# Softmax of grouped heads laid out by token tile, with folds in place of reduces and a direct SBUF spread; the last transpose of the first stage moved behind the paired Q chunks

## The chip, the cores and the metric

The kernel runs on one core of one Trainium2 chip. The metric is the device time of one execution in microseconds (us), as a median or mean of several executions.

Engine names: PE is TensorE (PEld its weight load), DVE is VectorE, ACT is ScalarE, POOL is GpSimd, SP is SyncE. An L number is a line of the kernel. L93 is a wrapper through which nearly all DVE, ACT and POOL operations pass, so these are told apart by their tile names. L118 holds nearly all matmuls; L213 (L219 in the changed kernel) holds those that transpose tiles. PSUM is the memory that matmuls write their sums to; an eviction is the DVE or ACT operation that reads such a sum out of it, so that the accumulator can be used again. The granted clock is the share of PE's full clock that the trace records.

## The reference

Two layers are applied to x of 2048 tokens by 1024 columns in bf16. Each is an attention block followed by a feed-forward block.

```
x = x + A(layernorm(x))     # 32 heads of 32; a query at s sees keys s, s-2, ..., s-14 (window 8, dilation 2)
                            # logits with negative key positions are -1e9; softmax over the 8; times V; times Wo
x = x + B(layernorm(x))     # gelu(x @ w1 + b1) @ w2 + b2, 1024 -> 3584 -> 1024
(both once more, with the same weights)
```

## The kernel before

The tokens go through in groups of 512, four per layer. The eight (layer, group) pairs are n = 0 to 7. For each n there are a QKV stage, a Wo stage and two FFN stages, all of them matmuls. They are interleaved so that DVE can do the attention of group n+2 while PE does the matmuls of group n. PE's program order is forced. `hold()` makes every later DVE instruction follow all that DVE was given up to now.

The first stage (n = 0) starts while its inputs still arrive. Four layer-norm tiles of 128 tokens must be transposed on PE. Tiles 2 and 3 come late, between paired Q chunks that need only tiles 0 and 1:

```python
# gen_qkv, n == 0: six chunks, each summed over k in four quarters kq, on tokens 0..255
for kq in range(4 if n == 0 else 0):
    for c in range(6):
        first[c] = qkv_chunk(wq, c, xnT, first.get(c), kq * (KD // 4), (kq + 1) * (KD // 4), 0, 2)
        if kq == 3:
            act.copy(qT[:, c, 0:2 * P], first[c][:, 0:2 * P])
        if (kq, c) in ((2, 5), (3, 1)):
            transpose_on_pe(*first_late.pop(0))     # 8 PE transposes into PSUM tile L, one ACT copy of 1024 columns
```

From group 2 on, the window logits of all heads are gathered by DMA into a tile with 128 partitions, partition = token tile * 32 + head. DVE then does the softmax. The weights `a` go to DRAM and come back spread over the head's dimensions:

```python
def gather(n):
    for tb in range(NTT):                                   # 4 transfers, each onto 32 partitions
        pool.dma_start(Lq[tb * H:(tb + 1) * H, :, :, :], prod[:, tb, :, :])

def attend(n):
    ...                                                     # e = sum of the four parts, 3 adds; mask where n % NG == 0
    vec.tensor_reduce(out=mx[:], in_=L[:].rearrange("p w t -> p t w"), axis=AX.X, op=ALU.max)
    vec.tensor_tensor(out=e[:], in0=L[:], in1=<mx for all w>, op=ALU.subtract)
    act.activation(e[:], e[:], ACT.Exp, scale=SCALE)
    vec.tensor_reduce(out=z[:], in_=e[:].rearrange("p w t -> p t w"), axis=AX.X, op=ALU.add)
    vec.reciprocal(z[:], z[:])
    vec.tensor_tensor(out=a[:], in0=e[:], in1=<z for all w>, op=ALU.mult)

def spread(n):
    for tb in range(NTT):
        pool.dma_start(a_d[:, :, tb * P:(tb + 1) * P], a[tb * H:(tb + 1) * H, :, :])   # SBUF -> DRAM
    for j in range(HP):
        pool.dma_start(abc[j::HP, :, :], a_d[:, :, :])                                 # DRAM -> SBUF

def av(n, c):          # abc * window of V, then three adds that fold 8 -> 4 -> 2 -> 1
    ...

# the stages from group 1 on (cut)
for n in range(1, N - 2):
    stage(gen_wo(n), ...)
    stage(gen_qkv(n + 2), sides=(at(0, spread, 2) if n == 1 else []) + each(av, n + 1, 0, 2, 0, 3))
    gather(n + 2)
    stage(gen_ffn1(n), ...)
    if n + 3 < N:
        stage(gen_ffn2(n), sides=at(0, attend, n + 2) + at(2, ln_a, n + 3))
    ...
```

The FFN2 stage sums four token tiles of one half of the output columns, then four of the other half. There are six PSUM accumulators, so the third tile of the second half needs that DVE has evicted the first tile of the first half.

## Time and profile before

| before | |
|---|---|
| time, median of 3 | 1233.33 us (1233.09 to 1233.33) |
| profiled span | 1231.1 us, granted clock 1.0 |
| PE busy | 1226.2 us (100%) |
| DVE busy | 870.0 us (71%) |

These are lines of the profile's page of before: busy time per engine, HBM traffic, the shares of the chain of work that ended last, and two groups of DMA transfers (count, size of one, median us from issue to landing).

```profile
PE 1226.2 (100%) x5789; PEld 632.7 (51%) x5789; DVE 870.0 (71%) x892; ACT 307.1 (25%) x491; POOL 123.0 (10%) x230
...
HBM read 197.40 MB, written 6.29 MB: 165 GB/s over the span
...
PE 99%; DVE 0%; DMA 0%; ACT 0%; issue 0%
...
abc<-a_d POOLq DMA_DIRECT2D x32, 256.0 KB, 5.0
big<-big POOLq DMA_DIRECT2D x24, 256.0 KB, 7.0
```

PE is the limit. One FFN stage is 224 matmuls of 512 columns in 48.35 us, 215.8 ns each. A group's matmuls come to 704 such units, so all eight groups need 8 x 704 x 0.2158 = 1215.4 us. This is an estimate from the trace, and the profiled span of the kernel before is only 1.3% above it. The Trainium skill, "TensorE: Matmul & The Clock Gate", section "Back-to-back issue gap", gives N/2.4 + 2.5 ns for a warm gap, 216 ns at N = 512, and the trace agrees.

The table of waits of before (engine and tile, what it waited for: us in total, times, longest us) leaves PE two:

```profile
DVE big L93 <- DMA abc<-a_d: 23.7, 2, 12.6
...
PE acc L118 <- DVE big L93: 1.1, 1, 1.1
...
PE L L213 <- ACT xnT L93: 0.7, 1, 0.7
```

The 1.1 us is the very first matmul waiting for its zeroed operand. The 0.7 us is the wait in the head of the kernel that the change goes for. It stands in the timeline of PE (start, duration, operation and count, in brackets the idle time before it and what ended that):

```profile
12.79 0.61 PE L213 MATMUL L<-ident,xn 128*128 128x128 bf16 x8
13.24 0.61 PE L118 MATMUL acc<-xnT,wt 128*128 128x256 bf16 x4
14.50 0.61 PE L213 MATMUL L<-ident,xn 128*128 128x128 bf16 x8 [0.66 <-ACT xnT L93]
14.94 2.90 PE L118 MATMUL acc<-xnT,wt 128*128 128x256 bf16 x25
```

Tile 2 is transposed at 12.79. Four chunk matmuls follow, and then the transposes of tile 3 must wait, because ACT has not yet copied tile 2 out of the PSUM tile L that both share. In the timeline of ACT, that copy runs from 13.44 to 14.45:

```profile
13.44 1.01 ACT L93 COPY xnT<-L 128x1024 bf16<-128x1024 bf16 x1 [0.97 <-PE L L213]
```

The groups of DVE instructions by shape (busy us, mean ns of one) show the two reduces of a softmax at 1.92 us each:

```profile
L93 DVE TENSOR_REDUCE z<-e 128x128 f32<-128x1024 f32 x8 | 15.4, 1926 | 33.7 <-ACT e L93 33.7
...
L93 DVE TENSOR_REDUCE mx<-e 128x128 f32<-128x1024 f32 x6 | 11.5, 1918 | 0.1
```

Four lines of the timeline of DVE before: two are the end of group 2's softmax and the first use of its spread weights. The other two are the start of the softmax in the first FFN2 stage with one, and that stage's first eviction:

```profile
281.54 1.20 DVE L93 TENSOR_TENSOR a<-e,z 128x1024 bf16<-128x1024 f32 x1
295.38 2.29 DVE L93 TENSOR_TENSOR big<-abc,vT 128x4096 bf16<-128x4096 bf16 x1 [12.64 <-DMA abc<-a_d]
...
365.65 1.22 DVE L93 TENSOR_TENSOR e<-big 128x1024 f32<-128x1024 bf16 x1
...
374.00 0.68 DVE L93 TENSOR_TENSOR tmp<-acc,b2bc 128x512 f32<-128x512 f32 x1
```

### The profile page before, as it was taken

The numbers are of one execution on the slowest core, as the hardware profiler recorded it, in microseconds if no ns is written. First come the engines' busy times: TensorE is split into PE (matmuls) and PEld (weight loads), VectorE is DVE, ScalarE is ACT, GpSimd is POOL, SyncE is SP. The second block draws the span as 40 slices with busy tenths as digits, with TensorE's granted clock in tenths as the row PEclk, the third lists the DMA queues.
The fourth block names the chain that finished last, engine by engine and source line by source line (L and its number), as shares of the span: only waits on it lengthen the run. The fifth ranks groups of instructions, "written<-read, shape, count | busy, mean of one in ns | idle before, by whom it ended". The sixth has DMA issues, their size and how long they took to land.

```text
span 1231.1 us, 13996 instructions
## 1 busy us (share of the span) xinstructions
PE 1226.2 (100%) x5789; PEld 632.7 (51%) x5789; DVE 870.0 (71%) x892; ACT 307.1 (25%) x491; POOL 123.0 (10%) x230
## 2 busy tenths in 40 slices
PE   9999999999999999999999999999999999999999
PEld 7666544456444564445544465444654444444444
DVE  8989899995996999376992779927599698012001
ACT  4343152014310143202431024310244101400310
POOL 3010011101021102200031000210000102000000
PEclk9999999999999999999999999999999999999999
DMA  9954677756487658756476565766666569546441
GB/s 301 289 179 142 177 220 183 210 140 230 147 197 226 177 165 180 220 170 186 149 187 222 172 171 169 174 222 196 171 183 157 186 200 198 166 158 196 153 136 53
DMA packets 219359, 226.63 MB, mean 184 GB/s; under 512 B 68562, under 2 KB 187488, under 8 KB 216224
## 3 DMA queue, kind: packets, MB, share of 16 engines
q1 hardware_dynamic: 214704, 208.69, 57.1%
q0 software_dynamic: 4592, 17.05, 5.7%
q8 instruction: 45, 0.74, 0.2%
q14 instruction: 18, 0.15, 0.0%
HBM read 197.40 MB, written 6.29 MB: 165 GB/s over the span
## 4 chain that ended last, share of the span: by engine, by line
PE 99%; DVE 0%; DMA 0%; ACT 0%; issue 0%
PE acc L118 99%; DMA x<-in_A_x_dram 0%; DVE stats L93 0%; PE acc L213 0%; PE L L118 0%; PE L L213 0%; ACT xnT L93 0%; DVE xn L93 0%; DVE x L93 0%; DVE mv L93 0%; PE acc L183 0%; DVE rstd L93 0%
## 5 line engine op out<-in xcount | busy, mean ns | idle before, releaser
L118 PE MATMUL acc<-xnT,wt 128*128 128x512 bf16 (+1 forms) x3392 | 720.8, 375 | 0.0
L118 PEld LDWEIGHTS <-wt 128*128 128x128 bf16 x3392 | 400.3, 119 | 318.8 <-issue 1.6
L118 PE MATMUL acc<-wt,hT 128*128 128x512 bf16 (+1 forms) x1820 | 388.1, 376 | 0.0
L118 PEld LDWEIGHTS <-hT 128*128 128x128 bf16 x1820 | 178.1, 98 | 209.0
L93 DVE TENSOR_TENSOR big<-big 128x2048 bf16<-128x2048 bf16 (+2 forms) x184 | 245.6, 1360 | 2.9
L93 ACT ACTIVATE hT<-acc,b1T 128x512 bf16<-128x512 f32 x224 | 152.5, 688 | 331.3 <-PE acc L118 331.2
L93 DVE TENSOR_TENSOR big<-qT,kT 128x4096 bf16<-128x4096 bf16 x64 | 143.8, 2286 | 26.7 <-ACT kT L93 26.1
L93 DVE TENSOR_TENSOR big<-abc,vT 128x4096 bf16<-128x4096 bf16 x64 | 144.8, 2287 | 24.3 <-DMA abc<-a_d 23.7
L93 DVE TENSOR_TENSOR tmp<-acc,b2bc 128x512 f32<-128x512 f32 x56 | 38.7, 690 | 148.4 <-PE acc L118 144.9
L93 ACT CAST qT<-acc 128x512 bf16<-128x512 f32 (+1 forms) x72 | 38.0, 542 | 341.4 <-PE acc L118 341.4
L118 PE MATMUL acc<-wt,oT 128*128 128x512 bf16 x448 | 97.9, 379 | 0.0
L93 DVE BATCH_NORM_STATS2 stats<-x 128x6 f32<-128x512 bf16 x128 | 83.5, 680 | 3.3 <-DMA x<-in_A_x_dram 2.6
L118 PEld LDWEIGHTS <-oT 128*128 128x128 bf16 x448 | 43.9, 98 | 52.8
L93 DVE TENSOR_TENSOR x<-acc,big 128x512 bf16<-128x512 f32 (+1 forms) x9 | 5.7, 633 | 90.0 <-PE acc L118 90.0
L93 POOL TENSOR_TENSOR rstd<-mv,eps_t 128x1 f32<-128x1 f32 x56 | 22.5, 402 | 434.4 <-DVE mv L93 434.3
L93 ACT CAST vT<-acc 128x512 bf16<-128x512 f32 x64 | 37.5, 586 | 83.1 <-PE acc L118 83.1
L93 ACT CAST kT<-acc 128x512 bf16<-128x512 f32 x64 | 37.3, 588 | 66.7 <-PE acc L118 66.6
L93 DVE TENSOR_TENSOR x<-acc,x 128x512 bf16<-128x512 f32 x64 | 42.6, 669 | 3.9 <-PE acc L118 3.8
L93 POOL TENSOR_TENSOR rstd<-rstd,mhalf 128x1 f32<-128x1 f32 x56 | 41.6, 743 | 4.4
L93 DVE TENSOR_SCALAR xn<-x,mv,rstd 128x1024 bf16<-128x1024 bf16 x52 | 28.4, 546 | 17.1 <-POOL rstd L93 16.9
L93 DVE TENSOR_TENSOR x<-tmp,x 128x512 bf16<-128x512 f32 x56 | 38.6, 690 | 1.6
L93 DVE TENSOR_REDUCE z<-e 128x128 f32<-128x1024 f32 x8 | 15.4, 1926 | 33.7 <-ACT e L93 33.7
(64 smaller groups left out, 252.0 us busy)
## 6 DMA issues: line engine op xcount, KB each, us to landing
wt<-in_B_w_dram SPq DMA_DIRECT2D x56, 1024.0 KB, 7.1
wt<-in_B_w_dram SPq DMA_DIRECT2D x64, 896.0 KB, 5.1
wt<-in_A_wqkv_dram SPq DMA_DIRECT2D x46, 1024.0 KB, 5.7
wt<-in_A_wo_dram SPq DMA_DIRECT2D x16, 1024.0 KB, 5.0
abc<-a_d POOLq DMA_DIRECT2D x32, 256.0 KB, 5.0
big<-big POOLq DMA_DIRECT2D x24, 256.0 KB, 7.0
x<-in_A_x_dram SPq DMA_DIRECT2D x16, 256.0 KB, 5.7
out_dram<-x SPq DMA_DIRECT2D x31, 128.0 KB, 2.4
```

Of the source, the lines that this page charges most:

```text
L93: inst = f(*args, **kwargs)
L118: return pe(nc.tensor.matmul(*args, **kwargs))
```

## The change

The intent is to take work and waits off DVE, the DMA queues and DRAM, and to close PE's gap in the head. The core of the diff (helpers and declarations are cut):

```diff
# 1. the head
@@ gen_qkv
-                if kq == 3:
-                    act.copy(qT[:, c, 0:2 * P], first[c][:, 0:2 * P])
-                if (kq, c) in ((2, 5), (3, 1)):
+                if (kq, c) in ((2, 5), (3, 5)):
+                    for done in range(2 if kq == 3 else 0):
+                        act.copy(qT[:, done, 0:2 * P], first[done][:, 0:2 * P])
                     transpose_on_pe(*first_late.pop(0))
+        for c in list(first)[2:]:
+            act.copy(qT[:, c, 0:2 * P], first[c][:, 0:2 * P])
# 2. partition = head * 4 + token tile, from group 2 on
@@ gather
-        for tb in range(NTT):
-            pool.dma_start(Lq[tb * H:(tb + 1) * H, :, :, :], prod[:, tb, :, :])
+        for j in range(HP):
+            pool.dma_start(Lq[:, j, :, :], prod[j::HP, :, :, :])
# 3. folds in place of reduces
+    def fold(e, op):
+        t = iop.tile([P, W // 2, P], F32, name="tmp")
+        vec.tensor_tensor(out=t[:], in0=e[:, 0:4, :], in1=e[:, 4:8, :], op=op)
+        vec.tensor_tensor(out=t[:, 0:2, :], in0=t[:, 0:2, :], in1=t[:, 2:4, :], op=op)
+        vec.tensor_tensor(out=t[:, 0, :], in0=t[:, 0, :], in1=t[:, 1, :], op=op)
+        return t[:, 0, :]
@@ attend
-        vec.tensor_reduce(out=mx[:], ...)                  # n < 2 keeps this one, which reads PSUM
+            mx = fold(L, ALU.max)
-        vec.tensor_reduce(out=z[:], ...)
-        vec.reciprocal(z[:], z[:])
+        vec.reciprocal(z[:], fold(e, ALU.add))
# 4. the spread, directly from SBUF to SBUF from group 2 on
@@ spread
+        if n < 2:
+            a_d = dram.tile(...)                           # groups 0 and 1 as before
+            ...
+            a = a_d
         for j in range(HP):
-            pool.dma_start(abc[j::HP, :, :], a_d[:, :, :])
+            pool.dma_start(abc[j::HP, :, :, :], a[:])
@@ av: abc is [P, NTT, W, P] now, so the adds are strided
-        vec.tensor_tensor(out=pv[:, 0:4, :], in0=pv[:, 0:4, :], in1=pv[:, 4:8, :], op=ALU.add)
+        vec.tensor_tensor(out=pv[:, :, 0:4, :], in0=pv[:, :, 0:4, :], in1=pv[:, :, 4:8, :], op=ALU.add)
# 5. one more hold
-            stage(gen_ffn2(n), sides=at(0, attend, n + 2) + at(2, ln_a, n + 3))
+            stage(gen_ffn2(n), sides=at(0, hold) + at(0, attend, n + 2) + at(2, ln_a, n + 3))
```

More of the change, by code (lines that the diff above doesn't have):

```diff
@@ L155 @@
     smat = const.tile([P, H], BF16, name="smat")
-    mask = const.tile([H, W - 1, HALO], F32, name="mask")
+    mask = const.tile([P, W - 1, HALO], F32, name="mask")
     khalo = const.tile([P, NCH, HALO], BF16, name="khalo")
@@ L171, in build_constants, with spread_mask @@
         for w in range(W - 1):
-            pool.memset(mask[:, w, 0:HALO - DIL * w], -1e9)
+            pool.memset(mask[0:H, w, 0:HALO - DIL * w], -1e9)
+    def spread_mask():
+        first = smp.tile([H, W - 1, HALO], F32, name="mx")
+        vec.tensor_copy(first[:], mask[0:H, :, :])
+        vec.memset(mask[:], 0.0)
+        pool.dma_start(mask[0::NTT, :, :], first[:])
     b1_rows = attp.tile([KF, P], BF16, name="abc")
@@ L267, in new_xnT @@
         return (pool or xnp).tile([P, NTT, KD, P], BF16, name="xnT")
-    def win(t_ap):
-        a = t_ap.ap
-        assert len(a) == 2 and a[1][0] == 1 and a[1][1] == HALO + T
-        return bass.AP(tensor=t_ap.tensor, offset=t_ap.offset, ap=[list(a[0]), [DIL, W], [1, T]])
     def win_by_tile(t_ap):
@@ L404, in attend @@
         if n % NG == 0:
-            vec.tensor_tensor(out=L[0:H, 0:W - 1, 0:HALO], in0=L[0:H, 0:W - 1, 0:HALO], in1=mask[:], op=ALU.add)
-        mx = smp.tile([P, P], F32, name="mx")
-        vec.tensor_reduce(out=mx[:], in_=L[:].rearrange("p w t -> p t w"), axis=AX.X, op=ALU.max)
-        vec.tensor_tensor(out=e[:], in0=L[:], in1=mx[:].unsqueeze(1).to_broadcast([P, W, P]), op=ALU.subtract)
+            p = H if n == 0 else P
+            vec.tensor_tensor(out=L[0:p, 0:W - 1, 0:HALO], in0=L[0:p, 0:W - 1, 0:HALO], in1=mask[0:p, :, :], op=ALU.add)
+        if n < 2:
+            mx = smp.tile([P, P], F32, name="mx")
+            vec.tensor_reduce(out=mx[:], in_=L[:].rearrange("p w t -> p t w"), axis=AX.X, op=ALU.max)
+            mx = mx[:]
+        else:
+            mx = fold(L, ALU.max)
+        vec.tensor_tensor(out=e[:], in0=L[:], in1=mx.unsqueeze(1).to_broadcast([P, W, P]), op=ALU.subtract)
         act.on = 1 < n < N - 1
@@ L412, in attend @@
         z = smp.tile([P, P], F32, name="z")
-        vec.tensor_reduce(out=z[:], in_=e[:].rearrange("p w t -> p t w"), axis=AX.X, op=ALU.add)
-        vec.reciprocal(z[:], z[:])
+        vec.reciprocal(z[:], fold(e, ALU.add))
         a = smp.tile([P, W, P], BF16, name="a")
@@ L422, in spread @@
         a = s.pop("a")
-        abc = attp.tile([P, W, T], BF16, name="abc")
+        abc = attp.tile([P, NTT, W, P], BF16, name="abc")
         s["abc"] = abc
         s["oT"] = attp.tile([P, NCH, T], BF16, name="qT" if n == N - 1 else "oT")
-        a_d = dram.tile([H, W, T], BF16, name="a_d")
-        for tb in range(NTT):
-            pool.dma_start(a_d[:, :, tb * P:(tb + 1) * P], a[tb * H:(tb + 1) * H, :, :])
+        if n < 2:
+            a_d = dram.tile([H, NTT, W, P], BF16, name="a_d")
+            for tb in range(NTT):
+                pool.dma_start(a_d[:, tb, :, :], a[tb * H:(tb + 1) * H, :, :])
+            a = a_d
         for j in range(HP):
-            pool.dma_start(abc[j::HP, :, :], a_d[:, :, :])
+            pool.dma_start(abc[j::HP, :, :, :], a[:])
     def av(n, c):
         s = st[n]
-        pv = bigp.tile([P, W, T], BF16, name="big")
-        vec.tensor_tensor(out=pv[:], in0=s["abc"][:], in1=win(s["vT"][:, c, :]), op=ALU.mult)
-        vec.tensor_tensor(out=pv[:, 0:4, :], in0=pv[:, 0:4, :], in1=pv[:, 4:8, :], op=ALU.add)
-        vec.tensor_tensor(out=pv[:, 0:2, :], in0=pv[:, 0:2, :], in1=pv[:, 2:4, :], op=ALU.add)
-        vec.tensor_tensor(out=s["oT"][:, c, :], in0=pv[:, 0, :], in1=pv[:, 1, :], op=ALU.add)
+        pv = bigp.tile([P, NTT, W, P], BF16, name="big")
+        vec.tensor_tensor(out=pv[:], in0=s["abc"][:], in1=win_by_tile(s["vT"][:, c, :]), op=ALU.mult)
+        vec.tensor_tensor(out=pv[:, :, 0:4, :], in0=pv[:, :, 0:4, :], in1=pv[:, :, 4:8, :], op=ALU.add)
+        vec.tensor_tensor(out=pv[:, :, 0:2, :], in0=pv[:, :, 0:2, :], in1=pv[:, :, 2:4, :], op=ALU.add)
+        o = s["oT"][:, c, :].rearrange("p (b t) -> p b t", t=P)
+        vec.tensor_tensor(out=o, in0=pv[:, :, 0, :], in1=pv[:, :, 1, :], op=ALU.add)
     def gen_wo(n):
@@ L594 @@
         stage(gen_qkv(n + 2), sides=(at(0, spread, 2) if n == 1 else []) + each(av, n + 1, 0, 2, 0, 3))
+        if n == 1:
+            spread_mask()
         gather(n + 2)
```

## The prediction

> **What bounds it.** TensorE. The busy table gives PE 1226.2 of 1231.1 us, the chain of waits is 99% PE matmuls, and the table of waits shows only two PE waits: 1.1 us at the start and 0.7 us before 14.50 us. In the timeline the 224 matmuls of 512 columns of one FFN half take 48.35 us (502.48 to 550.83), 216 ns each. The Trainium skill, "TensorE: Matmul & The Clock Gate", Part 2, has a matmul stream one column a cycle; 512 columns at its 2.4 GHz are 213 ns, and the trace agrees to about 1%. The change leaves the matmuls as they are, so shorter DVE, ACT or DMA work can gain no more than PE's gaps.
>
> **Head (on the chain).** PE waits 0.66 us for the ACT copy of tile 2 (13.44-14.45) before it may transpose tile 3. After the change PE first runs all twelve matmuls of the last quarter: 13.24 + 12 x 107 ns = 14.52, just as that copy ends. Transposes to 14.96, chunks 6 and 7 (16 x 107) to 16.67; before, that point was at 17.50. ACT's order after: copy of tile 2, four qT casts (0.28 us pitch), copy of tile 3 (1.01 us), which ends at about 16.6: just in time. Gain 0.83 us, less 0 to 0.2 if that copy is late.
>
> **The rest (off the chain).** Each TENSOR_REDUCE from SBUF (1.92 us) becomes a fold, about 1.25 us, estimated from the timed f32 adds (0.69 us for 512 columns). The Trainium skill, "VectorE: DVE Perf Modes", tier table, has reduce at 1x only; here the strided one from SBUF is slower still than that from PSUM (1.22 us). 14 folds save some 9 us of DVE. The DRAM detour: in group 2, a is done at 282.7 and the multiply starts at 295.4; about 4.3 us of that is the first hop, and with a itself some 3 us earlier DVE starts about 7 us sooner. The strided adds should cost what the contiguous ones do (1.22, 0.69, 0.42 us). PE waits for none of it.
>
> **What could become a wait.** The new hold in FFN2 pins 8 layer-norm statistics (0.60 us each) after the attention values, and the whole softmax now precedes FFN2's first evictions. In the first such stage (350.5-398.9 us) the softmax starts at about 357.5 (365.65 before); adds, statistics, norms, folds, exp and reciprocal sum to about 17 us, so the first eviction comes at about 374.3. PE needs it by 377.0 (before the third tile of the second half, 374.7 + 2 x 1.51). Slack 2.7 us. The two later stages have over 10. The hidden hiccup at 952.9 (0.15 us, ACT's exp delaying GELU) should shrink.
>
> **Prediction.** 1232.5 us, range 1231.8 to 1233.7; chances: faster by over 2% 0.01, within 2% 0.98, slower by over 2% 0.01.
>
> **What would show it.** The PE wait on the ACT copy gone, and all later stage starts 0.6-0.9 us earlier by the same amount. DVE busy down from 870 to about 860 us; no a_d transfer from group 2 on, the 12.6 us DVE idle before 295 down to about 8; HBM traffic about 8 MB lower; no new PE wait.
>
> **What would make it wrong.** The tile 3 copy late by over 0.8 us (ACT placing it after more casts), strided adds falling out of their fast mode (DVE would run past 377 us and stall PE by microseconds in three stages), or the SBUF-to-SBUF spread landing later than the DRAM route.

## The result, and the profile after

| | before | after |
|---|---|---|
| time, median | 1233.33 us (1232.86 to 1233.63, 6 runs) | 1232.80 us (1232.38 to 1233.17, 6 runs) |
| profiled span | 1231.1 us | 1230.8 us |
| granted clock | 1.0 | 1.0 |

The ratio is 0.9996, with a 95% interval of 0.9983 to 1.0009. Ratios here and below are over the fast runs of the same rounds. Executions over 1.5% slower than the fastest of the same kernel are left out of the means. They are not quite the ratios of the medians, nor always those of the means (x3_later has 0.9996, and 0.9998 from the means). The page of after, the lines that answer to those of before:

```profile
PE 1222.2 (99%) x5739; PEld 632.6 (51%) x5789; DVE 861.9 (70%) x922; ACT 307.3 (25%) x491; POOL 87.2 (7%) x207
...
HBM read 191.11 MB, written 4.72 MB: 159 GB/s over the span
...
PE 99%; DMA 1%; issue 0%; SPq 0%; DVE 0%
...
big<-big POOLq DMA_DIRECT2D x24, 256.0 KB, 3.6
abc<-a POOLq DMA_DIRECT2D x24, 256.0 KB, 5.3
```

PE's 4 us less is no gain: 50 of its 5789 matmul records are missing from this trace, and its first matmuls, which only warm PE up, took 1.34 us less (below). DVE has 8.1 us less. HBM moved 7.86 MB less. The gather's transfers (big<-big) land in 3.6 us in place of 7.0. Each of them now writes 128 partitions instead of 32, and reads every fourth of 128 partitions instead of all of them. That agrees with the Trainium skill, "SBUF — State Buffer", section "Can I just issue two DMAs to hit both halves?": "The only way to hit all 16 ports is one transfer spanning all 128 partitions." No run here varied the written partitions alone, so the cause of the 3.4 us less is argued, not shown.

The table of waits of after:

```profile
DVE big L93 <- DMA abc<-a: 13.4, 3, 5.8
...
PE acc L219 <- DVE xn L93: 1.5, 1, 1.5
...
PE acc L118 <- DMA wt<-in_A_wqkv_dram: 0.3, 1, 0.3
```

The 1.5 us are a real wait, but they cost nothing. PE's first transposes need DVE's first normalized tile, which comes at about the same time in both (transposes at 7.06 us in before, 7.15 in after). Ahead of them stand 14 warm-up matmuls, all of them in both traces. They start 427 ns apart, and 216 ns apart once the clock is granted in full: from 6.65 us in before, already from 3.92 us in after. So in after they end sooner, and the rest of the time is idle. PE's timeline in before, and then in after:

```profile
1.05 5.94 PE L118 MATMUL acc<-big 128*128 128x512 bf16 x14 [1.05 <-DVE big L93]
...
1.05 4.60 PE L118 MATMUL acc<-big 128*128 128x512 bf16 x14 [1.05 <-DVE big L93]
```

after_again, another execution of the same program, has 5.95 us there and 0.3 us of that wait. PE's wait for ACT is gone. In its place stands a wait of 0.3 us for weights (wt<-in_A_wqkv_dram). The timeline of PE in the head:

```profile
12.06 1.53 PE L118 MATMUL acc<-xnT,wt 128*128 128x256 bf16 x12 [0.33 <-DMA wt<-in_A_wqkv_dram]
13.43 0.61 PE L219 MATMUL L<-ident,xn 128*128 128x128 bf16 x8
13.88 1.48 PE L118 MATMUL acc<-xnT,wt 128*128 128x256 bf16 x12
15.20 0.61 PE L219 MATMUL L<-ident,xn 128*128 128x128 bf16 x8
```

From tile 2's transposes to the first head sum, no PE wait is left in this execution. In the timeline of ACT, the copy of tile 3 starts as soon as the four casts ahead of it are through, and no PE wait follows:

```profile
14.99 1.21 ACT L93 CAST qT<-acc 128x256 bf16<-128x256 f32 x4
16.04 1.07 ACT L93 COPY xnT<-L 128x1024 bf16<-128x1024 bf16 x1
```

But tile 2's transposes themselves start 0.64 us later than in before (13.43 against 12.79), because the weights ahead of them landed later in this execution. Count the head from that point, to the first head sum (the first matmuls of attention logits). Before needs 64.36 - 12.79 = 51.57 us, after 64.19 - 13.43 = 50.76, so 0.81 us less. The two start points hide most of it from a comparison by clock time.

The fold, by shape: 687 + 423 + 288 ns = 1.40 us, against 1.92 for a reduce.

```profile
L93 DVE TENSOR_TENSOR tmp<-e 128x512 f32<-128x512 f32 x14 | 9.6, 687 | 27.1 <-ACT e L93 27.1
...
L93 DVE TENSOR_TENSOR tmp<-tmp 128x256 f32<-128x256 f32 x14 | 5.9, 423 | 0.3
...
L93 DVE TENSOR_TENSOR tmp<-tmp 128x128 f32<-128x128 f32 x14 | 4.0, 288 | 0.3
```

The timeline of DVE, at the same four places as before:

```profile
278.76 1.22 DVE L93 TENSOR_TENSOR a<-e,z 128x1024 bf16<-128x1024 f32 x1
285.79 4.50 DVE L93 TENSOR_TENSOR big<-abc,vT 128x4096 bf16<-128x4096 bf16 x2 [5.81 <-DMA abc<-a]
...
354.40 1.22 DVE L93 TENSOR_TENSOR e<-big 128x1024 f32<-128x1024 bf16 x1
...
371.65 0.69 DVE L93 TENSOR_TENSOR tmp<-acc,b2bc 128x512 f32<-128x512 f32 x1
```

The spread costs DVE 5.8 us of idling instead of 12.6. DVE resumes 9.6 us sooner, and the FFN2 stage's first eviction ends at 372.34. PE needs it at 350.35 (stage start) + 24.17 (first half) + 14 x 0.2158 (two tiles of 7 matmuls) = 377.54. That leaves 5.2 us.

Finally the hiccup near 953 us. ACT serves one exp between GELUs, with two table loads. In before the first GELU after it starts at 952.55, as this line of ACT's timeline shows, and PE pauses for 0.15 us at 952.93:

```profile
952.55 3.00 ACT L93 ACTIVATE hT<-acc,b1T 128x512 bf16<-128x512 f32 x5
```

In after it starts at 951.38, and PE's stream has no pause there:

```profile
951.38 4.19 ACT L93 ACTIVATE hT<-acc,b1T 128x512 bf16<-128x512 f32 x7
```

The stretch between two stage starts of PE, from 198.6 to 958.5 us in before, takes 759.88 us in before and 759.74 in after. So the two gains inside the span are 0.81 and 0.14 us, together 0.95, and only 0.5 of them shows in the time.

**Where the rest is.** The measured time is longer than the profiled span, which starts with the first and ends with the last instruction of the program. The difference is nearly constant for one kernel, but not the same for both: 1.66 to 1.78 us in all executions of before whose span is listed, and 2.03 to 2.16 in all of after. The view of the DMA queues of after, from 1231 to 1234 us (its span ends at 1230.8), has one packet on the queue that carries instructions:

```profile
DMA packets 1, 0.01 MB, mean 3 GB/s; under 512 B 0, under 2 KB 0, under 8 KB 0
...
q14 instruction: 1, 0.01, 0.7%
```

The same view of before (its span ends at 1231.1) has none:

```profile
DMA packets 0, 0.00 MB, mean 0 GB/s; under 512 B 0, under 2 KB 0, under 8 KB 0
```

The packet is 8192 bytes, starts 1.64 us after the last instruction ended and takes 0.32 us. The changed program has 30 instructions more on DVE (922 against 892), and the packet seems to be a piece of that longer stream, fetched at the very end. The experiments below come back to it.

### The profile page after: what moved, and what is told of

Read it like the earlier page. It is cut to its first block, busy times and chain, and to the rows that moved or that the text cites. A ratio compares the mean times of both kernels' runs of the same rounds, so it can differ in the third digit from the quotient of the medians.

```text
span 1230.8 us, 13962 instructions
## 1 busy us (share of the span) xinstructions
PE 1222.2 (99%) x5739; PEld 632.6 (51%) x5789; DVE 861.9 (70%) x922; ACT 307.3 (25%) x491; POOL 87.2 (7%) x207
## 4 chain that ended last, share of the span: by engine, by line
PE 99%; DMA 1%; issue 0%; SPq 0%; DVE 0%
PE acc L118 98%; DMA wt<-in_A_wqkv_dram 1%; SPq L93 0%; PE L L118 0%; PE L L219 0%; DVE x L93 0%
## 5 line engine op out<-in xcount | busy, mean ns | idle before, releaser
L93 DVE TENSOR_TENSOR big<-big 128x1024 bf16<-128x1024 bf16 (+2 forms) x184 | 245.2, 1360 | 2.2
L93 POOL TENSOR_TENSOR rstd<-mv,eps_t 128x1 f32<-128x1 f32 x56 | 14.2, 253 | 515.4 <-DVE mv L93 509.4
L93 POOL DMA_DIRECT2D big<-big x24 | 13.3, 565 | 256.3 <-DVE big L93 237.6
L93 POOL TENSOR_TENSOR rstd<-rstd,mhalf 128x1 f32<-128x1 f32 x56 | 31.0, 553 | 4.4
```

Of the source, the lines that this page charges most:

```text
L93: inst = f(*args, **kwargs)
```

## The experiments

Three questions were open after the result. Is the head's 0.81 us real, and what takes part of it away again? The theory was that the gain is real but meets other arrivals (weights, DVE's products) that are nearly as late. The rivals were that the head saves less than counted, or that the rest of the change costs something. The second question is whether anything of the DVE work saved reaches the time. The theory was that none does, since DVE only has to keep its deadlines. The third came from comparing all runs: what lies outside the span. All 12 runs gave correct results. Where a quoted expectation speaks of a theory or a rival, it says itself what that one holds.

The measurements in one table: means over fast runs minus the mean of before in the same rounds, in us. "Outside" is time minus span. The last column says whether the profile shows an instruction packet after the span's end, and when it starts.

| kernel | chip | time | span | outside itself | late packet |
|---|---|---|---|---|---|
| before_again | 11 | -0.09 | -0.10 | 1.71 | none |
| after_again | 11 | -0.57 | -0.96 | 2.10 | +1.64 |
| head_only | 11 | -0.35 | -0.38 | 1.74 | none |
| rest_only | 11 | +0.22 | -0.18 | 2.10 | +1.60 |
| x3_later | 10 | -0.22 | -0.59 | 2.09 | +1.66 |
| fold_undone | 10 | -1.38 | -1.39 | 1.73 | none |
| delay_5 | 10 | -0.40 | -0.39 | 1.70 | none |
| delay_20 | 10 | +13.69 | +13.69 | 1.72 | none |
| after_third | 3 | -0.63 | -1.00 | 2.11 | +1.61 |
| before_loads | 3 | +0.75 | +0.78 | 1.71 | none |
| loads_moved | 3 | +0.46 | +0.49 | 1.71 | +1.12 |
| x3_only | 7 | -0.12 | -0.49 | 2.10 | +1.61 |

Before itself has 1.70 to 1.74 us outside on these four chips. The 95% intervals of the ratios are 0.0013 wide to each side, 1.6 us. So all verdicts but delay_20's rest on what the profiles show, not on the ratio alone.

### Both kernels again, unchanged: before_again, after_again, after_third

No edit. These give the scatter of one and the same program.

> The kernel before, unchanged, run as if it were a change: the scatter of this measurement. Both theories: ratio 1.0000, within 0.0005. Its profile shows again the PE wait of 0.66 us on the copy of tile 2 and the PE pause of 0.15 us near 953 us. Whether the arrival of the third weight piece (11.07 us in the first profile of before, 12.02 us in that of after) is the same again tells if that is scatter: if it is, some executions of before also show a PE wait on the weights near 11.5 us.

Measured: ratio 0.9999 (0.9987 to 1.0012), median 1233.10 us, profiled span 1231.4.

> The changed kernel, unchanged, once more, for its profile and a tighter ratio. Theory A (the head gains 0.83 us, the GELU pause 0.15 us, and late weights give some of it back in some executions): ratio 0.9992 to 0.9997 (0.4 to 1.0 us faster). If the weights land by 11.4 us in this execution, there is no PE wait near 11.5 us and the stage that starts at 64.36 us in before starts near 63.6 us. Rival B (the change itself delays the weights by 0.5 us): the wait near 11.5 us is there again, and the stage starts near 64.2 us.

Measured: ratio 0.9995 (0.9983 to 1.0008), median 1232.80 us, profiled span 1230.3.

> The changed kernel unchanged, beside these two: ratio 0.9994 to 0.9998; its profile shows another sample of where the weights land (third piece 11.1 to 12.3 us) and of PE's wait at 11.4 us, which should be about the landing time less 11.5 us plus 0.1.

Measured on another chip: ratio 0.9995 (0.9981 to 1.001), median 1232.61 us, profiled span 1230.5. Before had one outlier of 5968.93 us among these rounds.

What follows. From tile 2's transposes to the first head sum, the two profiles of before take 51.57 us each, and the three of after take 50.76 each. The head saves 0.81 us in all of these, in which PE waits for nothing else on this stretch. Where it does wait, for weights, the gain can be lost, as head_only will show. What varies is when tile 2's transposes begin: 12.79 and 13.14 in before; 13.43, 12.98 and 13.17 in after. That follows the landing of the third piece of Wq (11.07, 11.73; 12.02, 11.38, 11.75 us), which the change doesn't touch. Behind the first head sum, the program takes nearly the same time everywhere: 1166.7 us to the end with the layout of before (before, head_only, before_loads), 1166.6 with that of after (after, after_again, rest_only, fold_undone, x3_only). x3_later is an exception with 1166.9. So nearly the whole scatter of the span arises in the first 64 us.

In the span the gain is 0.96 us on chip 11 and 1.00 on chip 3, close to the two mechanisms' 0.81 + 0.14. In the time it is 0.57 and 0.63, and the difference is what lies outside the span.

### Head alone, the rest alone: head_only, rest_only

head_only is the kernel before with the diff's part 1; rest_only is the kernel after without it.

```diff
 # head_only, against before (rest_only: the same lines reverted in after)
-                if kq == 3:
-                    act.copy(qT[:, c, 0:2 * P], first[c][:, 0:2 * P])
-                if (kq, c) in ((2, 5), (3, 1)):
+                if (kq, c) in ((2, 5), (3, 5)):
+                    for done in range(2 if kq == 3 else 0):
+                        act.copy(qT[:, done, 0:2 * P], first[done][:, 0:2 * P])
                     transpose_on_pe(*first_late.pop(0))
+        for c in list(first)[2:]:
+            act.copy(qT[:, c, 0:2 * P], first[c][:, 0:2 * P])
```

> The kernel before with only the late transpose of tile 3. Theory A: nearly the whole gain, 0.4 to 0.85 us (ratio 0.9993 to 0.9997), the 0.66 us PE wait gone, the 0.15 us pause near 953 us still there. Rival (the gain comes from the 8 us less of DVE work and the shorter spread): ratio 1.0000, no gain.

Measured: ratio 0.9997 (0.9984 to 1.001), median 1233.26 us (1232.11 to 1233.52), profiled span 1231.7.

> The changed kernel with the transpose of tile 3 back in its old place. Theory A: 0.1 to 0.2 us faster than before (ratio 0.9999, not to be told from 1), the 0.66 us PE wait there, the pause near 953 us gone, DVE busy about 862 us all the same. Rival (DVE work counts): 0.3 us or more faster than before.

Measured: ratio 1.0001 (0.9987 to 1.0014), median 1233.59 us (1233.13 to 1234.01), profiled span 1231.9, DVE busy 861.7 us.

The hiccup goes with the rest of the change, not with the head: the stretch between the same two stage starts takes 759.88 us in head_only, as in before, and 759.73 in rest_only.

rest_only is the clearest case of what lies outside. Its span is 0.18 us shorter than before's, in line with the 0.14 us of the hiccup, though its five spans scatter by 0.9 us. Its time is 0.22 us longer, because it has 0.40 us more outside. Its profile also shows a wait for weights that has nothing to do with the new head. The next group's weights land at 53.93 us, and PE waits for them:

```profile
53.98 11.45 PE L118 MATMUL acc<-xnT,wt 128*128 128x512 bf16 x52 [0.60 <-DMA wt<-in_A_wqkv_dram]
```

head_only gained 0.38 us of span, of the 0.81. Its five spans are 1230.4, 1230.8, 1231.5, 1231.7 and 1231.8. The profile is of one of the long ones, and PE's timeline there shows two waits for weights:

```profile
12.18 1.53 PE L118 MATMUL acc<-xnT,wt 128*128 128x256 bf16 x12 [0.49 <-DMA wt<-in_A_wqkv_dram]
...
26.01 2.16 PE L118 MATMUL acc<-xnT,wt 128*128 128x512 bf16 x9 [0.47 <-DMA wt<-in_A_wqkv_dram]
```

The first is the third Wq piece again, which delays either kernel. The second is a price of the earlier head. The second half of the K weights landed at 25.96 us, 12.41 us after tile 2's transposes began. With the old order PE asks for it 12.64 us after that point, with the new one 11.82 us after. In nine more profiles it landed 10.84 to 12.35 us after that point: 11.21 and 12.23 in the two of before, 10.88 to 11.42 in the three of after, 12.35 in delay_5, whose PE waited there too. So in executions where these weights land late, the new head gives most of its gain back: head_only's profile takes 51.46 us from tile 2's transposes to the first head sum, which leaves 0.11 of the 0.81. (delay_5 takes 52.07, since it also waited 0.46 us near 54 us, where rest_only did.) head_only and the rest together gained 0.56 us of span against 0.96 for the whole. Whether head_only met late weights more often by chance isn't settled by five runs.

### Moving the load of tile 3: x3_later

If the third Wq piece delays PE at 11.4 us, the load of x tile 3 could let it pass.

```diff
-        if k < 4:
-            load_x(0, 2 + k // 2, 3 + k // 2)
+        if k in (0, 4):
+            load_x(0, 2 + k // 4, 3 + k // 4)
```

> The changed kernel with the load of the fourth x tile put behind the third weight piece instead of ahead of it. Theory A: the third piece lands about 0.7 us sooner (the time that a 256 KB load holds the queue), so no PE wait near 11.5 us in any execution; the fourth x tile is still in time (it is needed at about 12 us). Ratio to before 0.9990 to 0.9995, so 0 to 0.5 us faster than the changed kernel. Rival: the fourth tile's normalisation becomes late and PE waits before transposing it: no gain, or 0.5 us slower.

Measured: ratio 0.9996 (0.9983 to 1.001), median 1233.56 us (1233.19 to 1234.41), profiled span 1232.3. The third weight piece (11.80 us) no longer held PE, but the rival was right. DVE works in program order, and the statistics of tile 3 stand there ahead of the normalizing of tile 2. Tile 3 landed at 12.48 us, and PE then waited for tile 2 instead. The timeline of PE:

```profile
14.70 0.62 PE L219 MATMUL L<-ident,xn 128*128 128x128 bf16 x8 [1.33 <-DVE xn L93]
```

### The folds undone: fold_undone

The two reduces come back in after; layout and spread stay.

```diff
-        if n < 2:
+        if True:
             mx = smp.tile([P, P], F32, name="mx")
 ...
-        vec.reciprocal(z[:], fold(e, ALU.add))
+        vec.tensor_reduce(out=z[:], in_=e[:].rearrange("p w t -> p t w"), axis=AX.X, op=ALU.add)
+        vec.reciprocal(z[:], z[:])
```

> The changed kernel with tensor_reduce back in all softmaxes. DVE busy rises by about 8 us to about 870. Theory A: at most 0.15 us slower than the changed kernel, by the pause near 953 us coming back: ratio to before 0.9994 to 0.9998. Rival (DVE work is felt): several us slower than the changed kernel.

Measured: ratio 0.9989 (0.9976 to 1.0001), median 1232.49 us (1231.95 to 1232.75), profiled span 1230.8, DVE busy 870.0 us. All of DVE's saving is thus the folds', and it is worth nothing in time. The profile has no pause near 953 us either: the stretch from 198.6 to 958.5 takes 759.73 us here. So the folds are not needed for the hiccup to go; another part of the change suffices, and which one stays open. Counted from the first head sum, the softmax's last subtraction ahead of the exp ends after 884.45 us in before, 884.11 here and 883.45 in after.

The kernel was faster than the range expected, and part of this miss has its cause outside the span: with fewer DVE instructions it has no late packet, and 1.73 us outside instead of 2.10. The remaining 0.4 us of span, against the -0.96 and -1.00 of after on two other chips, is not explained. Before was 0.5 us slower on this chip than on the others, and after itself wasn't run on it.

### How much room DVE has: delay_5, delay_20

Five or twenty additions of 0.72 us that nothing needs are put on DVE ahead of the first evictions of that FFN2 stage.

```diff
+    def delay(n):
+        if n > 1:
+            return
+        junk = iop.tile([P, HALF], F32, name="tmp")
+        vec.on = True
+        vec.memset(junk[:], 0.0)
+        for _ in range(5):                    # delay_20: 20
+            vec.tensor_tensor(out=junk[:], in0=junk[:], in1=junk[:], op=ALU.add)
+        vec.on = False
+        vec.hold()
...
-            stage(gen_ffn2(n), sides=at(0, hold) + at(0, attend, n + 2) + at(2, ln_a, n + 3))
+            stage(gen_ffn2(n), sides=at(0, hold) + at(0, attend, n + 2) + at(2, ln_a, n + 3) + at(2, delay, n))
```

> The changed kernel with five idle f32 adds of 128x512 (and one memset; about 4 us of DVE in all) put ahead of the first evictions of the second FFN2 stage, where the first eviction ended at 372.3 us and PE needs it at 377.5 us. Theory A (5.2 us of slack there): no PE wait, time as the changed kernel's, ratio to before 0.9994 to 0.9998. Rival (DVE time is felt at once): 4 us slower, ratio 1.003.

Measured: ratio 0.9997 (0.9983 to 1.001), median 1233.75 us of 4 runs (1232.07 to 1234.04). The first eviction in DVE's timeline now ends at 378.88:

```profile
378.19 0.69 DVE L93 TENSOR_TENSOR tmp<-acc,b2bc 128x512 f32<-128x512 f32 x1
```

This execution ran 1.56 us behind the profile of after at that point (the waits for weights), so PE's need is at 377.54 + 1.56 = 379.1. PE did not wait. The eviction moved by 4.98 us against its stage, so the slack is at least that; 0.2 us were left of the 5.2 counted.

> The same with twenty idle adds, about 15 us of DVE. Theory A: the first eviction ends near 387.2 us, PE waits for it from 377.5 us, about 9.7 us, and perhaps 2 to 3 us more for the second eviction, as the scheduler now puts a multiply between them; 9.5 to 12.5 us slower than the changed kernel, ratio to before 1.007 to 1.010, and no other PE wait later. Rival (PE never waits for DVE here because six accumulators are enough): ratio below 1.001.

Measured: ratio 1.0111 (1.0097 to 1.0125), median 1247.81 us, above the expected 1.007 to 1.010. PE's timeline has the two waits for DVE, of which the first begins at 388.02 - 10.36 = 377.66, where the count has PE's need:

```profile
388.02 3.15 PE L118 MATMUL acc<-wt,hT 128*128 128x512 bf16 x7 [10.36 <-DVE tmp L93]
392.56 7.71 PE L118 MATMUL acc<-wt,hT 128*128 128x512 bf16 x25 [1.39 <-DVE tmp L93]
```

The stage is 63.83 us long instead of 48.35, so 15.48 longer, but the two waits come to only 11.75, or 12.34 counted from start to start of the matmuls around them. The other 3.1 us are 16 matmuls after the waits that run at about half speed. The busy time by stretch tells the rest (stretch, its length; busy us of PE, PEld, DVE, ACT and POOL; granted clock, DMA share, GB/s):

```profile
350.00:377.50 27.50, 27.34 (x126) 12.45 (x127) 26.05 (x43) 3.03 (x3) 5.29 (x12) 1.00 0.72 198
377.50:388.00 10.50, 0.16 (x1) 0.00 (x0) 9.95 (x16) 0.00 (x0) 0.00 (x0) 0.76 0.33 131
388.00:397.00 9.00, 7.58 (x19) 2.64 (x19) 9.00 (x9) 0.00 (x0) 0.00 (x0) 0.53 0.06 9
397.00:398.00 1.00, 1.00 (x7) 0.44 (x5) 1.00 (x2) 0.00 (x0) 0.00 (x0) 1.00 0.63 172
```

The idle PE lost its clock: 0.5 of it was granted from 382.86 to 396.52 us, and the matmuls after the wait came 427 ns apart instead of 216. That agrees with the Trainium skill, "TensorE: Matmul & The Clock Gate", Part 1, by which at least one idle window of about 3.4 us puts the array back to half clock; here it came 5.2 us after PE stopped. The expectation had left it out. A deadline missed by 10.4 us thus cost the stage 15.5 us. (The 13.69 us of the table are against before, which lacks after's gain.)

### Weights ahead of other loads: loads_moved, before_loads

loads_moved is after with tile 3 loaded later, its statistics behind the normalizing of tile 2 (which takes away the wait of x3_later), and the x tiles of groups 2 and 3 loaded behind the K weights. before_loads is the same on before.

```diff
-        if k < 4:
-            load_x(0, 2 + k // 2, 3 + k // 2)
+        if k in (0, 4):
+            load_x(0, 2 + k // 4, 3 + k // 4)
...
-        stats(2)
-        stats(3)
         for tt in range(2, 4):
+            stats(tt)
             first_late.append((norm(tt), xa[0][:, tt, :, :], both[:, tt - 2, :, :]))
...
         wk = load_qkv(1)
+        if n < 2:
+            load_x(n + 2)                     # and the two earlier load_x(2), load_x(3) taken out
```

> The changed kernel with three loads moved back in the queue: the fourth x tile behind the third weight piece (and tile 2 normalised before tile 3's statistics, so that it doesn't wait for that load), x tiles 8 to 11 behind the K weights, x tiles 12 to 15 behind the next group's weights. Theory A (the head's 0.82 us is partly given back because PE then meets weights still in flight at 11.4, 25.2 and 53 us): no PE wait on weights at any of the three, from tile 2's transpose to the first head sum 50.76 us in the profile, ratio to before 0.9989 to 0.9994, 0.2 to 0.6 us faster than the changed kernel. Rival (those waits are not what takes the gain): ratio as the changed kernel's, 0.9995 to 0.9997.

Measured: four runs from 1232.50 to 1235.80 us, ratio 1.0004 (0.999 to 1.0018), and one of 3376.41. The profile fell into that last one, so how its head ran can't be read; this stays open.

> The kernel before with the same three loads moved. Theory A: PE still waits 0.66 us for the copy of tile 2 (51.57 us from tile 2's transpose to the first head sum), waits on weights are gone: 0 to 0.4 us faster than before, ratio 0.9997 to 1.0000. Rival: as large a gain as the moved loads give the changed kernel.

Measured: ratio 1.0006 (0.9993 to 1.0019), median 1233.98 us (1233.33 to 1235.21), profiled span 1232.0. The weights came earlier (third Wq piece 10.06 us, second half of K 21.75), and no wait for weights is left in its profile. But the x tiles of group 2 came later. DVE stood idle for them, as DVE's timeline shows:

```profile
22.43 1.28 DVE L93 BATCH_NORM_STATS2 stats<-x 128x6 f32<-128x512 bf16 x2 [1.27 <-DMA x<-in_A_x_dram]
```

It then finished the products for the first head sum late, and PE waited there:

```profile
65.29 0.61 PE L118 MATMUL L<-big,smat 128*32 128x512 bf16 x8 [0.59 <-DVE big L93]
```

So a third chain ends close to the first head sum. In before, DVE is done 1.56 us ahead of PE there (62.80 against 64.36). After the change it is 0.44, 0.64 and 0.46 us in the three profiles.

### Tile 3 alone: x3_only

After with the first two hunks of loads_moved only; the x tiles of later groups stay where they were.

> The changed kernel with the fourth x tile loaded behind the third weight piece and tile 2 normalised before tile 3's statistics; no other load moved. Theory A (at the head three chains run within half a microsecond of each other: PE, the weight loads, and DVE on its way to the first head sum, which in the changed kernel ends 0.3 to 0.6 us before PE needs it): the third piece lands 0.7 us sooner and PE's wait at 11.4 us is gone, but DVE reaches the next group's statistics up to 0.3 us later and PE may wait for it at the first head sum near 63.6 us; net 0 to 0.4 us faster than the changed kernel, ratio to before 0.9992 to 0.9996. Rival (only the wait at 11.4 us takes the gain): no wait at the head sum and ratio 0.9990 to 0.9993.

Measured: ratio 1.0 (0.9987 to 1.0014), median 1233.19 us (1232.52 to 1233.72), profiled span 1230.4. In the profile, the third Wq piece landed at 10.71 us, the wait at 11.4 us is gone, and tile 2's transposes began at 12.86. The first head sum came at 63.86. That is 51.00 us after tile 2's transposes, 0.24 more than in after, and it was DVE that held it: its last product ended 0.15 us before, as in before_loads. That is no better than after's best (63.74), and the mean of its spans (-0.49 against before) is worse than after's. The three chains are seen, the gain in time isn't. No version was found that clearly beats after. fold_undone has the lowest times, but the intervals don't separate it.

### What lies outside the span

This uses all the runs together. In all profiles with an instruction packet that starts 1.60 to 1.66 us after the span's end (after, after_again, after_third, rest_only, x3_later, x3_only), the time outside was 2.03 to 2.12 us. In all without one, and in loads_moved, whose packet came half a microsecond sooner, it was 1.69 to 1.76.

delay_5 tells most. It is after with a few DVE instructions added and differs from it on no other engine by instruction count. The last 8 KB instruction packet, which comes at 1232.4 us in after, comes at 1134.0 in delay_5, inside the span, and the time outside is 1.70 us. delay_20, with 943 DVE instructions, has it inside the span too. The pages count 18 packets on that queue inside the span with 892 to 922 DVE instructions and 19 in these two; fold_undone, back at 894, has 18 and none after it. So the packet goes with the length of DVE's instruction stream, and whether it falls into the tail depends on the number of DVE instructions. That it makes the time longer is supported by association in 14 profiles and by these accidental tests, but not shown by a run made for it: after with one or two idle DVE instructions was not run. How it would do so stays open. The packet ends 1.96 to 2.19 us after the span, but the time outside does not follow that end: in x3_later the packet ends (2.19) when the 2.11 us outside are already over.

## Why the prediction was right or wrong, point by point

The time was predicted at 1232.5 us (1231.8 to 1233.7) and "within 2%" at 0.98. It came out at 1232.80. The range also held before's own 1233.33, so the time alone would have fitted no gain at all; what tests the prediction are the points below. That it is off by only 0.3 us is in part luck: two terms that it did not count have opposite signs.

- "TensorE bounds it, and shorter DVE, ACT or DMA work can gain no more than PE's gaps": right. fold_undone gave the 8.1 us of DVE work back and lost nothing.
- "Gain 0.83 us" in the head: right, 0.81 in the profiles of before and after. The copy of tile 3 came in time. What the prediction left out is that weights which land late can take most of it back (head_only).
- "All later stage starts 0.6 to 0.9 us earlier by the same amount": wrong as a check. The first head sum was 0.17 us earlier in the first pair of profiles, 0.98 in the second (64.72 and 63.74). The start of an execution varies by more than the gain with the landing of the first weights. The step that failed is taking two clock times of single executions as comparable.
- "No new PE wait": wrong in the letter. Waits for weights near 11.4 us come and go in both kernels. The one near 26 us is new with the earlier head where K's weights land late, 0.47 and 0.41 us in head_only and delay_5, and none in after's three profiles. One near 54 us came with the old head (rest_only, 0.60) as with the new one (delay_5, 0.46).
- The sum of the time: inside the span the gain was 0.96 to 1.00 us, with the hiccup's 0.14, which the prediction named but didn't add. What it had no term for is 0.38 us more outside the span, which goes with the late instruction packet. 0.81 + 0.14 - 0.38 = 0.57, and 0.5 to 0.6 were measured.
- "Each fold about 1.25 us": mis-sized, 1.40 by the shapes' means. The small third step costs 288 ns for a quarter of the first step's elements, which cost 687.
- "Strided adds cost what the contiguous ones do": right, 1219, 685 and 415 ns against 1220, 686 and 417.
- "DVE resumes about 7 us sooner, idle 12.6 down to about 8": mis-sized, 9.6 us and 5.8. a came 2.8 us earlier, and the way from a to the multiply got 6.8 us shorter, against the 4.3 estimated for the first hop.
- "Softmax of FFN2 at 357.5, slack 2.7 us": mis-sized on the safe side, 354.40 and 5.2 us, since DVE arrived earlier. delay_5 confirms the 5.2.
- DVE down to about 860 us and HBM traffic about 8 MB lower: right, 861.9 us and 7.86 MB. The hiccup at 952.9: gone, and the fold was not needed for it.

## What to carry to other kernels

When one engine is busy 99% of the span, count only its own gaps: work saved elsewhere buys slack, which is worth something only where a deadline would otherwise be missed (there 10.4 us late cost 15.5 us, also because PE lost its clock). A chain shortened by 0.8 us soon meets the next ones, here two that were 0.4 to 1.6 us behind it. For effects below a microsecond, measure between two events of the same chain rather than by the clock of the execution, and compare the time with the span, since what is gained inside can be lost outside.

## What the Trainium skill lacked or had wrong

- "Runtime: NRT & Kernel Launch", section "Instruction fetch mechanics", calls the cost of crossing an instruction block "mostly hidden". At the program's end it may not be: an 8192-byte packet 1.6 us after the last instruction goes with 2.10 us outside the span instead of 1.72 (an association; see above). The page speaks of 16 KiB blocks; the packets on this queue are of 8192 bytes.
- "TensorE: Matmul & The Clock Gate", section "Back-to-back issue gap", gives about 131 ns per matmul of 512 columns as the sustained rate of a stream with weight loads, and says that N/2.4 + 2.5 over-counts there. Here such a stream runs at 215.8 ns throughout, which is what that formula gives.
- "VectorE: DVE Perf Modes", section "The perf-mode tier table", has reduce at 1x whatever the source. Here a strided f32 reduce of 1024 columns took 1.92 us from SBUF and 1.22 us from PSUM, the latter as long as a plain f32 operation of that size.
- "DMA: Bandwidth & Descriptors" gives mean rates and no scatter. The first 512 KB weight piece landed 6.49 to 8.43 us after the start in 13 profiles that begin nearly alike; that scatter is larger than the whole effect studied here.
- No page that was read gives a cause for two outliers, 3376.41 us and 5968.93 us, on one chip. In the profiled one, most matmuls came some 620 ns apart. Its trace holds no clock record, so the clock of 1.0 that is printed for it says nothing.
